# Strassen's seven products for some of mm1's ff tiles in the later chunks of a fused attention and MLP kernel

## Chip, cores, metric

One core of one Trainium2 chip. The metric is the device time of one execution in microseconds (us). "Span" is the time from the first to the last instruction in the profile; it is some 1.8 us shorter than the time of the same run (before: 305.5 and 307.26). PE is TensorE, ACT ScalarE, DVE VectorE, POOL GpSimd; PEld are PE's weight loads.

## The reference, cut

```python
def _attn_ref(q, k, v):                 # B, H, S, D = 8, 8, 576, 64
    scores = scale * np.matmul(q, k.transpose(0, 1, 3, 2))
    # heads 0-3: the last 32 positions; heads 4-7: every fourth of the last 128
    scores = np.where(masks[None, :, :, :], scores, -1000000000.0)
    ...                                 # softmax, then attn @ v
def _moe_ref(x, w_in, w_out):           # x: 4608 x 512, w_in: 512 x 2048, w_out: 2048 x 512
    h = x @ w_in
    r = np.maximum(h, 0.0)
    return ((r * r) @ w_out).astype(np.float32)
```

## The kernel before: what the argument touches

The tokens are worked in nine chunks of 512 (0 to 8). For each chunk, mm1 makes 16 "ff tiles" of h (each 128 features by 512 tokens: four matmuls of 512 columns), ACT takes the relu and DVE the square. mm2 already uses Strassen's scheme: seven products of half-size blocks, with sums of g (`sm`) and of the weights (`T`) as operands. Each chunk's work is a generator; `pump(n)` issues n of its steps. The attention of batch b is issued between the steps of chunk b - 1 (batches 2 to 7 with chunks 1 to 6), so the numbers in `pump` set the order of everything on all engines. Chunks 7 and 8 have no attention beside them.

```python
def mm1_gen(c, g, sm=None):                      # two steps for each ff tile: 32
    for ffc in range(NFF):
        ph = pmool.tile([P, TOKC], FP32, ...)    # one of 4 PSUM banks
        for n, dmk in enumerate((2, 3, 0, 1)):
            nc.tensor.matmul(ph, wi[:, dmk, ffc * P : ffc * P + P], xs[:, dmk, :], ...)
            if n == 1:
                yield
        relu_squared(c, ffc, g, ph, rts)         # ACT relu -> rt, DVE rt * rt -> g (two tiles at a time)
        ...                                      # hidden_sums: DVE, 4 operations for each half of g
        yield

def mm2_strassen_gen(c, g, sm):                  # a product is 16 matmuls of 256 columns: 4 steps
    ...
    yield from product(a, gv[:, :, 0, 0:HT], B11, True)
    s1 = part("s1")
    nc.scalar.copy(s1, a)                        # ACT reads a's bank
    yield
    d_ = bank("pod")
    yield from product(d_, gv[:, :, 1, HT:TOKC], T[:, 3], True)
    yield
    b_ = bank("pob")
    yield from product(b_, sm[:, 1], T[:, 1], True)      # needs hidden sums
    ...

for b in range(2, B):
    pending.append(moe_gen(b - 1))
    pump(1)
    ...
    pump(11)                                     # (b == 2: weight sums instead)
    for g in range(2):
        s_sliding_x(b, g)                        # scores, exponentials (ACT), masks (DVE)
        pump(7 if b == 2 and g else 5)
    s_dilated(b, 0)
    pump(5 if b == 2 else 7)
    s_dilated(b, 1)
    ...
    pump(1 if b == 2 else 6)
    cast_v(nc.scalar)                            # ACT: v to f16, vp 1.49 us, then vd twice 1.07
    ...
    pump(3)
    attn_values(b, lambda: pump(2))              # PE: AT x vp, AT x vd
    pump(1000)
```

The softmax here doesn't subtract the row's maximum and nothing guards it: scores larger than these inputs give would overflow.

Of the kernel before, what the change touches and what calls it, by code (L numbers as in the profile page):

```python
# [8 lines left out]
FP16 = mybir.dt.float16  # L9
FP32 = mybir.dt.float32  # L10
I16 = mybir.dt.int16
ALU = mybir.AluOpType
ACTF = mybir.ActivationFunctionType
P = 128
# [3 lines left out]
def kernel(  # L18
# [9 lines left out]
    nc = tc.nc  # L28

    B, H, S, D = q.shape  # L30
# [6 lines left out]
    NDM = DM // P  # L37
    NFF = DFF // P
    scale = float(1.0 / (D ** 0.5))
    TOKC = 512  # L40
    NTOKC = NTOK // TOKC
# [6 lines left out]
    PADP = P - QB  # L48
# [6 lines left out]
    const = ctx.enter_context(tc.tile_pool(name="const", bufs=1))  # L55
# [2 lines left out]
    xp = ctx.enter_context(tc.tile_pool(name="xp", bufs=4))  # L58
    gp = ctx.enter_context(tc.tile_pool(name="gp", bufs=1))
    tp = ctx.enter_context(tc.tile_pool(name="tp", bufs=1))  # L60
    osb = ctx.enter_context(tc.tile_pool(name="osb", bufs=4))
    otp = ctx.enter_context(tc.tile_pool(name="otp", bufs=3))
    papool = ctx.enter_context(tc.tile_pool(name="papool", bufs=2, space=bass.MemoryType.PSUM))
    pmool = ctx.enter_context(tc.tile_pool(name="pmool", bufs=4, space=bass.MemoryType.PSUM))
    dpool = ctx.enter_context(tc.tile_pool(name="dpool", bufs=2, space=bass.MemoryType.DRAM))
# [5 lines left out]
    xT = const.tile([P, NDM, NTOK], FP16, name="xT")  # L71
# [2 lines left out]



    QKTp = [const.tile([P, 2, PADP + S], FP16, name=f"QKTp{hp}") for hp in range(2)]
    QKTd = const.tile([P, 2, 2, KPAD + S], FP16, name="QKTd")
    QKTx = const.tile([P, 2, PADP + HH * S], FP16, name="QKTx")
    AT = const.tile([P, 8, 640], FP16, name="AT")  # L80
# [235 lines left out]
    HT = TOKC // 2  # L316
    HM = DM // 2
    NK = NFF // 2
# [19 lines left out]
    def hidden_sums(g, sm, i0, i1):  # L338
        v = g_of(g)[:, i0:i1]
        a11, a12 = v[:, :, 0, 0:HT], v[:, :, 1, 0:HT]  # L340
        a21, a22 = v[:, :, 0, HT:TOKC], v[:, :, 1, HT:TOKC]
        s1, s2, s3, s4 = (sm[:, i, i0:i1, :] for i in range(4))
        yield nc.vector.tensor_add(s1, a21, a22)
        yield nc.vector.tensor_sub(s2, s1, a11)
        yield nc.vector.tensor_sub(s3, a11, a21)
        yield nc.vector.tensor_sub(s4, a12, s2)
# [35 lines left out]
    def mm1_gen(c, g, sm=None):  # L382
        xs = xT[:, :, c * TOKC : (c + 1) * TOKC]
        rts = {}
        for ffc in range(NFF):
            ph = pmool.tile([P, TOKC], FP32, name=f"ph{c}_{ffc}", tag="pm")
            for n, dmk in enumerate((2, 3, 0, 1)):
                nc.tensor.matmul(  # L388
                    ph,
                    wi[:, dmk, ffc * P : ffc * P + P],  # L390
                    xs[:, dmk, :],
                    start=(n == 0),
                    stop=(n == NDM - 1),
                )
                if n == 1:
                    yield
            relu_squared(c, ffc, g, ph, rts)
            if sm is not None and ffc >= NFF // 2:
                if ffc == NFF // 2:
                    sums = hidden_sums(g, sm, 0, NK // 2)  # L400
                if ffc == NFF - 1:
                    sums = hidden_sums(g, sm, NK // 2, NK)
                for _ in sums:
                    if ffc < NFF - 1:
                        break
            yield

    def mm2(c, g, po, t, ffc):
        nc.tensor.matmul(  # L409
            po,  # L410
            g[:, ffc, t * P : (t + 1) * P],
            wo[:, ffc, :],
            start=(ffc == 0),
            stop=(ffc == NFF - 1),
        )
# [12 lines left out]
    def mm2_strassen_gen(c, g, sm):  # L428
        gv = g_of(g)
        T = wsum["T"]  # L430
        last = c == NTOKC - 1

        def bank(name):
            return pmool.tile([P, 2, HM], FP32, name=f"{name}{c}", tag="pm")

        def half_product(acc, lhs, rhs, t, first):
            for k in range(NK):
                nc.tensor.matmul(  # L438
                    acc,
                    lhs[:, k, t * P : (t + 1) * P],  # L440
                    rhs[:, k, :],
                    start=(first and k == 0),
                    stop=(k == NK - 1),
                    skip_group_check=True,
                )
                if k % 4 == 3 and (t, k) != (1, NK - 1):
                    yield

        def product(acc, lhs, rhs, first):
            for t in range(2):  # L450
                yield from half_product(acc[:, t, :], lhs, rhs, t, first and t == 0)

        def part(name):
            return osb.tile([P, 2, HM], FP32, name=f"{name}{c}", tag="u")

        def put(half, ot, eng, cols=slice(0, DM)):
            rows = out[c * TOKC + half * HT : c * TOKC + (half + 1) * HT, cols]
            eng.dma_start(out=rows.rearrange("(t p) m -> p t m", p=P), in_=ot[:, :, cols])  # L458

        out_eng = nc.gpsimd if c < B - 1 else nc.sync  # L460
        left, right = slice(0, HM), slice(HM, DM)
        otu = otp.tile([P, 2, DM], FP32, name=f"otu{c}", tag="ot2")
        otl = otp.tile([P, 2, DM], FP32, name=f"otl{c}", tag="ot2")
        a = bank("poa")
        yield from product(a, gv[:, :, 0, 0:HT], B11, True)
        s1 = part("s1")
        nc.scalar.copy(s1, a)
        yield
        d_ = bank("pod")
        yield from product(d_, gv[:, :, 1, HT:TOKC], T[:, 3], True)  # L470
        yield
        b_ = bank("pob")
        yield from product(b_, sm[:, 1], T[:, 1], True)
        u2 = part("u2")
        nc.vector.tensor_add(u2, b_, s1)
        yield
        yield from product(a, gv[:, :, 1, 0:HT], B21, False)
        nc.scalar.copy(otu[:, :, left], a)  # L478
        if last:
            put(0, otu, nc.sync, left)  # L480
        yield
        yield from product(b_, sm[:, 2], T[:, 2], False)
        u3 = part("u3")
        nc.vector.tensor_add(u3, b_, s1)
        nc.vector.tensor_add(otl[:, :, left], d_, u3)
        if last:
            put(1, otl, nc.sync, left)
        yield
        c_ = bank("poc")
        yield from product(c_, sm[:, 0], T[:, 0], True)  # L490

        nc.vector.tensor_add(u2, c_, u2)
        nc.vector.tensor_add(otl[:, :, right], c_, u3)  # L493
        put(1, otl, out_eng, right if last else slice(0, DM))
        yield
        if last:
            for t, eng in ((0, nc.sync), (1, nc.scalar)):
                e_ = bank(f"poe{t}_")
                yield from half_product(e_[:, 0, :], sm[:, 3], B22, t, True)
                nc.vector.tensor_add(otu[:, t, right], e_[:, 0, :], u2[:, t, :])  # L500
                r0 = c * TOKC + t * P
                eng.dma_start(out=out[r0 : r0 + P, right], in_=otu[:, t, right])
        else:
            e_ = bank("poe")
            yield from product(e_, sm[:, 3], B22, True)
            nc.vector.tensor_add(otu[:, :, right], e_, u2)
            put(0, otu, out_eng)
        yield
# [20 lines left out]
    def moe_gen(c):  # L529
        g = hidden(c)  # L530
        sm = gp.tile([P, 4, NK, HT], FP16, name=f"sm{c}", tag="sm")
        yield from mm1_gen(c, g, sm)
        yield from mm2_strassen_gen(c, g, sm)


# [6 lines left out]
    def pump(n):  # L542
        for _ in range(n):
            while pending:
                try:
                    next(pending[0])
                    break
                except StopIteration:
                    pending.pop(0)
# [430 lines left out]
# [4 lines that stand above are left out]
        if b < B - 1:  # L984

            for i in range(2):
                nc.gpsimd.tensor_copy(hold, QKTx[:, i, PADP + HH * S - 2 : PADP + HH * S - 1])
                nc.gpsimd.tensor_copy(hold, QKTd[:, i, 1, KPAD + S - 1 :])
        if 2 < b < B - 1:
            dk = keep_qk(b + 1)  # L990
        if b == 2:
            for rows, ot in late:
                nc.gpsimd.dma_start(out=rows, in_=ot)
            dk = keep_qk(b + 1)
            for _ in weight_sums():
                pump(2)
        else:
            pump(11)
        for g in range(2):
            s_sliding_x(b, g)  # L1000
            pump(7 if b == 2 and g else 5)
        s_dilated(b, 0)
        pump(5 if b == 2 else 7)
        s_dilated(b, 1)
        if b + 1 < B:
            transpose_by_dma(dk)
        pump(1 if b == 2 else 6)
        cast_v(nc.scalar)
        if b + 1 < B:
            load_v(b + 1)  # L1010
        pump(3)
        attn_values(b, lambda: pump(2))
        pump(1000)
    for c in range(B - 1, NTOKC):
# [32 lines left out]
```

## Time and profile before

| | before |
|---|---|
| time, median of 3 runs | 306.73 us (306.72 to 307.37) |
| span of the profiled run | 305.5 us, clock 1.000 |
| TensorE (PE) busy | 97% |
| chunks 2 to 6 (with attention), each | 30.87 to 30.89 us |
| chunk 7 / chunk 8 to its last matmul | 26.04 / 26.20 us |

The chunk lengths are read off the timeline: from the start of a chunk's first mm1 matmul to that of the next chunk's. The page's lines stand in the prediction.

### The profile page before, as it was taken

What the parts mean: (1) busy time and instruction counts of PE and PEld (TensorE: products, weight loads), DVE (VectorE), ACT (ScalarE), POOL (GpSimd) and SP (SyncE); (2) the same over time, 40 slices, a digit from 0 to 9 for tenths busy, and PEclk for the clock granted to TensorE, in tenths of its full rate; (3) what the DMA queues carried; (4) which work ended last, traced back from release to release, by engine and by line L of the source; (5) the groups of instructions that cost most, each with busy time, mean ns of one, the idle gap of its engine ahead of it and who ended that gap; (6) DMA issues with size and microseconds to landing.
All of it is one profiled execution on the core that took longest, in us unless ns stands there. A gap on an engine that the chain in (4) does not pass through costs nothing.

```text
span 305.5 us, 7013 instructions
## 1 busy us (share of the span) xinstructions
PE 296.3 (97%) x2898; PEld 192.8 (63%) x2898; DVE 208.8 (68%) x410; ACT 185.0 (61%) x308; POOL 48.5 (16%) x97
## 2 busy tenths in 40 slices
PE   8899998999999999999999999999999999999994
PEld 3675444444696469646964697459745974684584
DVE  4653475849966797679766977697769775843744
ACT  6466777478834893489348943894389437405610
POOL 7454013006004100320032003200100010000000
PEclk9999999999999999999999999999999999999999
DMA  8999989899899998689939983989310012003004
GB/s 175 226 213 230 233 174 203 160 232 269 210 191 219 310 170 185 217 182 198 228 111 197 216 184 123 213 184 209 117 72 0 2 61 78 2 0 137 2 0 138
DMA packets 85615, 47.89 MB, mean 157 GB/s; under 512 B 68112, under 2 KB 82896, under 8 KB 85200
## 3 DMA queue, kind: packets, MB, share of 16 engines
q1 hardware_dynamic: 76688, 27.24, 40.8%
q0 software_dynamic: 8352, 19.80, 28.9%
q8 instruction: 22, 0.36, 0.5%
q10 hardware_dynamic: 544, 0.43, 0.5%
q14 instruction: 9, 0.07, 0.1%
HBM read 39.85 MB, written 16.52 MB: 184 GB/s over the span
## 4 chain that ended last, share of the span: by engine, by line
PE 90%; ACT 3%; DMA 3%; POOL 2%; issue 1%; DVE 1%; ACTq 0%; POOLq 0%
PE ph L388 42%; PE pob L438 9%; PE poa L438 9%; PE poe L438 5%; PE poc L438 5%; PE pod L438 4%; PE po L409 4%; DMA early<-in_q_dram 3%; PE paw L776 3%; PE pav L759 2%; PE pz L675 2%; PE ps L656 1%; PE py L809 1%; PE px L791 1%; POOL early L119 1%; ACT AT L628 1%
## 5 line engine op out<-in xcount | busy, mean ns | idle before, releaser
L388 PE MATMUL ph<-xT,wi 128*128 128x512 f16 x576 | 129.8, 379 | 0.0
L354 ACT ACTIVATE rt<-ph 128x512 f16<-128x512 f32 x144 | 84.9, 601 | 36.4 <-PE ph L388 36.1
L388 PEld LDWEIGHTS <-wi 128*128 128x128 f16 x576 | 54.4, 98 | 62.4
L358 DVE TENSOR_TENSOR g<-rt 128x1024 f16<-128x1024 f16 x63 | 43.5, 691 | 47.2 <-ACT rt L354 47.0
L438 PEld LDWEIGHTS <-sm 128*128 128x128 f16 x512 | 46.9, 98 | 4.8
L438 PEld LDWEIGHTS <-g 128*128 128x128 f16 x384 | 35.9, 98 | 6.9 <-DVE g L356 1.3
L438 PE MATMUL pob<-T,sm 128*128 128x256 f16 x256 | 32.5, 272 | 0.0
L438 PE MATMUL poa<-wo,g 128*128 128x256 f16 x256 | 32.4, 273 | 0.0
L458 POOL DMA_DIRECT2D out_dram<-otl x6 | 4.6, 763 | 152.6 <-DVE otl L493 152.6
L815 ACT COPY xT<-py 128x576 f16<-128x576 f16 x16 | 10.2, 640 | 27.3 <-PE py L809 27.3
L740 DVE TENSOR_TENSOR x_d<-paw,rcp_d 72x512 f16<-72x512 f32 x32 | 22.0, 687 | 1.1
L797 ACT COPY xT<-px 128x576 f16<-128x576 f16 x16 | 10.3, 642 | 13.6 <-PE px L791 13.6
L409 PE MATMUL po<-wo,g 128*128 128x512 f16 x64 | 17.8, 379 | 0.0
L735 DVE RECIPROCAL rcp_d<-paw 72x8 f32<-72x8 f32 x32 | 6.4, 199 | 16.2 <-PE paw L776 16.2
L628 ACT ACTIVATE AT<-pz 128x576 f16<-128x576 f32 x28 | 16.6, 652 | 1.0 <-PE pz L675 0.6
L628 ACT ACTIVATE AT<-ps 128x576 f16<-128x576 f32 x28 | 16.6, 649 | 0.5
L740 DVE TENSOR_TENSOR x_p<-pav,rcp_p 96x512 f16<-96x512 f32 (+1 forms) x24 | 16.2, 676 | 0.8
L438 PE MATMUL poe<-wo,sm 128*128 128x256 f16 x128 | 16.3, 273 | 0.0
L438 PE MATMUL pod<-T,g 128*128 128x256 f16 x128 | 16.3, 272 | 0.0
L438 PE MATMUL poc<-T,sm 128*128 128x256 f16 x128 | 16.2, 272 | 0.0
L478 ACT COPY otu<-poa 128x512 f32<-128x512 f32 x8 | 4.7, 586 | 17.5 <-PE poa L438 17.5
L629 DVE TENSOR_TENSOR AT<-AT,maskd 128x576 f16<-128x576 f16 x28 | 12.2, 455 | 3.5 <-ACT AT L628 2.5
(120 smaller groups left out, 354.5 us busy)
## 6 DMA issues: line engine op xcount, KB each, us to landing
sv<-in_v_dram SPq DMA_DIRECT2D x40, 128.0 KB, 3.1
sd<-in_v_dram SPq DMA_DIRECT2D x8, 512.0 KB, 6.2
dk<-in_k_dram POOLq DMA_DIRECT2D x12, 288.0 KB, 7.0
dk<-in_q_dram POOLq DMA_DIRECT2D x12, 288.0 KB, 7.5
out_dram<-otl POOLq DMA_DIRECT2D x6, 512.0 KB, 3.3
out_dram<-otu POOLq DMA_DIRECT2D x6, 512.0 KB, 4.2
sd<-in_v_dram SPq DMA_DIRECT2D x8, 288.0 KB
wi<-in_moe_w_in_dram POOLq DMA_DIRECT2D x4, 512.0 KB, 10.3
```

The lines of the kernel that those rows point to most:

```text
L354: nc.scalar.activation(rt[:, o, :], ph[:], ACTF.Relu)
L358: nc.vector.tensor_mul(g[:, ffc - 1 : ffc + 1, :], rt, rt)
L388: nc.tensor.matmul(ph, wi[:, dmk, ffc * P : ffc * P + P], xs[:, dmk, :], start=(n == 0), stop=(n == NDM - 1),)
L409: nc.tensor.matmul(po, g[:, ffc, t * P : (t + 1) * P], wo[:, ffc, :], start=(ffc == 0), stop=(ffc == NFF - 1),)
L438: nc.tensor.matmul(acc, lhs[:, k, t * P : (t + 1) * P], rhs[:, k, :], start=(first and k == 0), stop=(k == NK - 1), skip_group_check=True,)
L628: nc.scalar.activation(AT[:, u, 0:UW], ps[:, :, 0 : UW // 2], ACTF.Exp, scale=scale)
L629: nc.vector.tensor_mul(AT[:, u, 0:UW], AT[:, u, 0:UW], mask)
L735: nc.vector.reciprocal(rcp[0:w, 0:n], pv[:, :, :, D])
L740: nc.vector.tensor_tensor(out=x[0:w, 0:n], in0=pv[:, :, :, 0:D], in1=rcp[0:w, 0:n].unsqueeze(3).to_broadcast([w, n, HH, D]), op=ALU.mult,)
L776: nc.tensor.matmul(pav[:, e, h * (D + 2) : h * (D + 2) + D + 1], AT[:, u, off : off + P], vd[:, t, 2 * a + e, h, 0 : D + 1], start=True, s ...
L797: nc.scalar.copy(xT[:, 0:2, t0 : t0 + 288], px[:, 0:UW].rearrange("x (c t) -> x c t", c=2),)
L815: nc.scalar.copy(xT[:, 2:4, t0 : t0 + 288].rearrange("x c (i r) -> x c i r", r=DIL), py[:, 0:UW].rearrange("x (c r i) -> x c i r", c=2, r= ...
```

## The change

Its intent: a unit of Strassen's seven products computes four ff tiles from 28 matmuls of 256 columns in place of 16 of 512, one eighth fewer columns. Chunks 3 to 6 get one unit each (a quarter of their tiles), chunks 7 and 8 two. The price is sums of x and of the weights, and the combining of products, on DVE and ACT. Cut to its core (allocations left out, lines joined):

```diff
+    units = {**{c: 1 for c in range(3, NTOKC - 2)}, NTOKC - 2: 2, NTOKC - 1: 2}
+    # w_in_sums: 8 DVE operations, once, in chunk 2; x_sums(c): 4 DVE operations (t1..t4) per chunk
+    def unit_gen(c, u, g):
+        product(a, w(0, 0), x_quarter(c, 0, 0), True)
+        m1 = part("m1"); nc.scalar.copy(m1, a)
+        yield
+        product(e, w(0, 1), x_quarter(c, 1, 0), True)
+        nc.vector.tensor_add(g1[:, :, first], e, m1)
+        yield "stage"
+        product(a, s2, t2, False)                          # goes on adding in bank a
+        m6 = part("m6"); nc.scalar.copy(m6, a)
+        yield
+        product(d, s1, t1, True)
+        finish(g1[:, :, first])                            # ACT relu, DVE square, in place
+        yield "stage"
+        product(a, s3, t3, False)
+        m7 = part("m7"); nc.scalar.copy(m7, a)
+        nc.vector.tensor_add(g2[:, :, second], d, m7)
+        yield "stage"
+        product(a, w(1, 1), t4, False)
+        nc.scalar.activation(g2[:, :, first], a, ACTF.Relu)
+        yield
+        product(d, s4, x_quarter(c, 1, 1), False)          # must wait for the addition d + m7
+        nc.vector.tensor_mul(g2[:, :, first], g2[:, :, first], g2[:, :, first])
+        nc.vector.tensor_add(g1[:, :, second], d, m6)
+        yield "stage"
+        finish(g2[:, :, second]); finish(g1[:, :, second])
+
+    orders = {                       # 0, 1: a stage of that unit; p: a plain tile; s: one hidden sum
+        1: "0p0p0p0p0" + "p" + "sp" * 4 + "ppp",
+        2: "p01010p10p10p1psspspsp",
+    }
     ... chunk 7's mm2 takes its sixth and fifth products later; output buffers 3 -> 2
-            pump(11)
+            pump(14 if b - 1 in units else 11)
     ...
-        pump(1 if b == 2 else 6)
+        pump(1 if b == 2 else 5 if b - 1 in units else 6)
         cast_v(nc.scalar)
     ...
-        pump(3)
+        pump(1 if b - 1 in units else 3)
         attn_values(b, lambda: pump(2))
```

More of the change, by code (lines that the diff above doesn't have):

```diff
@@ L60 @@
     tp = ctx.enter_context(tc.tile_pool(name="tp", bufs=1))
+    kp = ctx.enter_context(tc.tile_pool(name="kp", bufs=1))
     osb = ctx.enter_context(tc.tile_pool(name="osb", bufs=4))
-    otp = ctx.enter_context(tc.tile_pool(name="otp", bufs=3))
+    otp = ctx.enter_context(tc.tile_pool(name="otp", bufs=2))
     papool = ctx.enter_context(tc.tile_pool(name="papool", bufs=2, space=bass.MemoryType.PSUM))
@@ L73 @@
     wo = wpool.tile([P, NFF, DM], FP16, name="wo")
-    QKTp = [const.tile([P, 2, PADP + S], FP16, name=f"QKTp{hp}") for hp in range(2)]
+    QKTp = [kp.tile([P, 2, PADP + S], FP16, name=f"QKTp{hp}", tag=f"k{hp}") for hp in range(2)]
     QKTd = const.tile([P, 2, 2, KPAD + S], FP16, name="QKTd")
@@ L406, in mm1_gen, with w_in_sums, quarter @@
             yield
+    units = {**{c: 1 for c in range(3, NTOKC - 2)}, NTOKC - 2: 2, NTOKC - 1: 2}
+    HU = 2 * P
+    ws = [const.tile([P, 4, 2, HU], FP16, name=f"ws{u}") for u in range(2)]
+    def w_in_sums(u):
+        def quarter(i, j):
+            f0 = 4 * P * u + HU * i
+            return wi[:, 2 * j : 2 * j + 2, f0 : f0 + HU]
+        s1, s2, s3, s4 = (ws[u][:, i] for i in range(4))
+        yield nc.vector.tensor_add(s1, quarter(1, 0), quarter(1, 1))
+        yield nc.vector.tensor_sub(s2, s1, quarter(0, 0))
+        yield nc.vector.tensor_sub(s3, quarter(0, 0), quarter(1, 0))
+        yield nc.vector.tensor_sub(s4, quarter(0, 1), s2)
@@ new lines, with x_quarter, x_sums @@
+    xsums = {}
+    def x_quarter(c, j, i):
+        t0 = c * TOKC + HT * i
+        return xT[:, 2 * j : 2 * j + 2, t0 : t0 + HT]
+    def x_sums(c):
+        t = [kp.tile([P, 2, 2, HT], FP16, name=f"xs{c}_{n}", tag=f"k{n}") for n in range(2)]
+        t1, t2, t3, t4 = t[0][:, 0], t[0][:, 1], t[1][:, 0], t[1][:, 1]
+        xsums[c] = t1, t2, t3, t4
+        nc.vector.tensor_sub(t1, x_quarter(c, 0, 1), x_quarter(c, 0, 0))
+        nc.vector.tensor_sub(t2, x_quarter(c, 1, 1), t1)
+        nc.vector.tensor_sub(t3, x_quarter(c, 1, 1), x_quarter(c, 0, 1))
+        nc.vector.tensor_sub(t4, x_quarter(c, 1, 0), t2)
@@ new lines, in unit_gen, with w, product, part @@
+    def unit_gen(c, u, g):
+        t1, t2, t3, t4 = xsums[c]
+        s1, s2, s3, s4 = (ws[u][:, i] for i in range(4))
+        f0 = 4 * u
+        g1, g2 = g[:, f0 : f0 + 2, :], g[:, f0 + 2 : f0 + 4, :]
+        first, second = slice(0, HT), slice(HT, TOKC)
+        def w(i, j):
+            c0 = P * f0 + HU * i
+            return wi[:, 2 * j : 2 * j + 2, c0 : c0 + HU]
+        def product(acc, lhs, rhs, start):
+            for n in range(2):
+                for k in range(2):
+                    nc.tensor.matmul(
+                        acc[:, n, :],
+                        lhs[:, k, n * P : (n + 1) * P],
+                        rhs[:, k, :],
+                        start=(start and n == 0 and k == 0),
+                        stop=(k == 1),
+                        skip_group_check=True,
+                    )
+        def part(name):
+            return osb.tile([P, 2, HT], FP32, name=f"{name}{c}_{u}", tag="u")
+        a = papool.tile([P, 2, HT], FP32, name=f"pu{c}_{u}", tag="pa")
+        def finish(x):
+            nc.scalar.activation(x, x, ACTF.Relu)
+            nc.vector.tensor_mul(x, x, x)
+        product(a, w(0, 0), x_quarter(c, 0, 0), True)
+        m1 = part("m1")
+        nc.scalar.copy(m1, a)
+        yield
+        e = pmool.tile([P, 2, HT], FP32, name=f"pe{c}_{u}", tag="pm")
+        product(e, w(0, 1), x_quarter(c, 1, 0), True)
+        nc.vector.tensor_add(g1[:, :, first], e, m1)
+        yield "stage"
+        product(a, s2, t2, False)
+        m6 = part("m6")
+        nc.scalar.copy(m6, a)
+        yield
+        d = pmool.tile([P, 2, HT], FP32, name=f"pq{c}_{u}", tag="pm")
+        product(d, s1, t1, True)
+        finish(g1[:, :, first])
+        yield "stage"
+        product(a, s3, t3, False)
+        m7 = part("m7")
+        nc.scalar.copy(m7, a)
+        nc.vector.tensor_add(g2[:, :, second], d, m7)
[7 more added lines that the diff above has]
+        yield "stage"
+        finish(g2[:, :, second])
+        finish(g1[:, :, second])
@@ new lines, with mm1_units_gen @@
+    orders = {
+        1: "0p0p0p0p0" + "p" + "sp" * 4 + "ppp",
+        2: "p01010p10p10p1psspspsp",
+    }
+    def mm1_units_gen(c, g, sm, nu):
+        if c not in xsums:
+            x_sums(c)
+        xs = xT[:, :, c * TOKC : (c + 1) * TOKC]
+        rts = {}
+        stages = [unit_gen(c, u, g) for u in range(nu)]
+        sums = hidden_sums(g, sm, 0, NK // 2)
+        ffc = 4 * nu
+        for step in orders[nu]:
+            if step == "p":
+                ph = pmool.tile([P, TOKC], FP32, name=f"ph{c}_{ffc}", tag="pm")
+                for n in range(NDM):
+                    nc.tensor.matmul(
+                        ph,
+                        wi[:, n, ffc * P : ffc * P + P],
+                        xs[:, n, :],
+                        start=(n == 0),
+                        stop=(n == NDM - 1),
+                    )
+                    if n == 1:
+                        yield
+                relu_squared(c, ffc, g, ph, rts)
+                ffc += 1
+                yield
+            elif step == "s":
+                next(sums)
+            else:
+                for what in stages[int(step)]:
+                    yield
+                    if what:
+                        break
+        assert ffc == NFF
+        for _ in sums:
+            pass
+        for _ in hidden_sums(g, sm, NK // 2, NK):
+            pass
+        yield
@@ L471, in mm2_strassen_gen, with sixth, fifth @@
         yield
-        b_ = bank("pob")
-        yield from product(b_, sm[:, 1], T[:, 1], True)
-        u2 = part("u2")
-        nc.vector.tensor_add(u2, b_, s1)
-        yield
+        def sixth():
+            b_ = bank("pob")
+            yield from product(b_, sm[:, 1], T[:, 1], True)
+            u2 = part("u2")
+            nc.vector.tensor_add(u2, b_, s1)
+            yield
+            return b_, u2
+        def fifth(u2):
+            c_ = bank("poc")
+            yield from product(c_, sm[:, 0], T[:, 0], True)
+            nc.vector.tensor_add(u2, c_, u2)
+            return c_
+        relaxed = c == NTOKC - 2
+        if not relaxed:
+            b_, u2 = yield from sixth()
         yield from product(a, gv[:, :, 1, 0:HT], B21, False)
@@ L481, in mm2_strassen_gen @@
         yield
+        if relaxed:
+            b_, u2 = yield from sixth()
+            c_ = yield from fifth(u2)
+            yield
         yield from product(b_, sm[:, 2], T[:, 2], False)
@@ L487, in mm2_strassen_gen @@
             put(1, otl, nc.sync, left)
-        yield
-        c_ = bank("poc")
-        yield from product(c_, sm[:, 0], T[:, 0], True)
-        nc.vector.tensor_add(u2, c_, u2)
+        if not relaxed:
+            yield
+            c_ = yield from fifth(u2)
         nc.vector.tensor_add(otl[:, :, right], c_, u3)
         put(1, otl, out_eng, right if last else slice(0, DM))
+        if c + 1 == NTOKC - 1:
+            x_sums(c + 1)
         yield
@@ L531, in moe_gen @@
         sm = gp.tile([P, 4, NK, HT], FP16, name=f"sm{c}", tag="sm")
-        yield from mm1_gen(c, g, sm)
+        if c in units:
+            yield from mm1_units_gen(c, g, sm, units[c])
+        else:
+            yield from mm1_gen(c, g, sm)
         yield from mm2_strassen_gen(c, g, sm)
@@ L996 @@
                 pump(2)
+        elif b == 3:
+            for u in range(2):
+                for _ in w_in_sums(u):
+                    pump(1)
+            pump(3)
         else:
-            pump(11)
+            pump(14 if b - 1 in units else 11)
         for g in range(2):
```

## The prediction

> **What bounds the kernel now.** I read the page's busy shares and its chain first. TensorE (PE) is busy for 97% of the span, and the chain that ended last is PE for 90%.
>
> ```profile
> PE 296.3 (97%) x2898; PEld 192.8 (63%) x2898; DVE 208.8 (68%) x410; ACT 185.0 (61%) x308; POOL 48.5 (16%) x97
> PE 90%; ACT 3%; DMA 3%; POOL 2%; issue 1%; DVE 1%; ACTq 0%; POOLq 0%
> ```
>
> Then I cut the span at the chunk borders that the chain in order of time shows, and asked for each engine's busy time per chunk:
>
> ```profile
> 156.88:187.76 30.88, 30.88 (x318) 20.78 (x316) 23.53 (x45) 20.24 (x33) 4.64 (x10) 1.00 0.79 182
> 249.50:275.54 26.04, 26.04 (x178) 17.23 (x176) 14.75 (x23) 10.72 (x18) 1.45 (x2) 1.00 0.11 41
> ```
>
> The first is chunk 4 with batch 5's attention beside it; the second is chunk 7, which has no attention. The columns are the stretch, its length, then busy time of PE, PEld, DVE, ACT and POOL, granted clock and DMA share. PE never rests in either, so matmul columns removed there come off the time one for one, and any new PE wait is added one for one. DVE has 7 us to spare beside attention, ACT 10.6. How fast PE runs comes from the chain in order of time:
>
> ```profile
> 249.50 13.81 PE ph L388 x64
> 263.32 1.75 PE poa L438 x16
> ```
>
> A 512-column matmul takes 13.81/64 = 0.2158 us, a 256-column one 1.75/16 = 0.1092 us.
>
> Since other engines must feed PE, I took the durations of their operations from the groups by shape (busy us, mean ns):
>
> ```profile
> L354 ACT ACTIVATE rt<-ph 128x512 f16<-128x512 f32 x144 | 84.9, 601 | 36.4 <-PE ph L388 36.1
> L358 DVE TENSOR_TENSOR g<-rt 128x1024 f16<-128x1024 f16 x63 | 43.5, 691 | 47.2 <-ACT rt L354 47.0
> L356 DVE TENSOR_TENSOR g<-rt 128x512 f16<-128x512 f16 x18 | 7.5, 424 | 1.8 <-ACT rt L354 1.2
> L475 DVE TENSOR_TENSOR u<-pob,s 128x512 f32<-128x512 f32 x8 | 5.5, 691 | 3.2 <-PE pob L438 3.2
> ```
>
> Last the order in time where attention's values start, in chunk 4:
>
> ```profile
> 170.75 0.43 PE L675 MATMUL pz<-QKTd 64*128 64x72 f16 x16
> 171.10 1.19 ACT L628 ACTIVATE AT<-pz 128x576 f16<-128x576 f32 x2
> 172.18 1.09 ACT L354 ACTIVATE rt<-ph 128x512 f16<-128x512 f32 x2
> 172.43 2.02 PE L438 MATMUL poa<-wo,g 128*128 128x256 f16 x16
> 173.13 1.49 ACT L166 CAST vp<-sv 128x1536 f16<-128x1536 f32 x1
> 174.29 1.04 PE L438 MATMUL pod<-T,g 128*128 128x256 f16 x8
> 175.16 0.42 PE L759 MATMUL pav<-vp,AT 128*128 128x65 f16 x8
> 176.39 0.62 ACT L467 COPY s<-poa 128x512 f32<-128x512 f32 x1
> ```
>
> The cast of v ends at 174.62, 0.54 us before PE wants it at 175.16. The copy of s1 runs at 176.39, though its product was done at 174.29: ACT keeps the program's order. In chunk 1, where the last scores stand closer to the values, the cast is already late:
>
> ```profile
> 80.99 1.47 ACT L166 CAST vp<-sv 128x1536 f16<-128x1536 f32 x1
> 82.52 0.42 PE L759 MATMUL pav<-vp,AT 128*128 128x65 f16 x8 [0.66 <-ACT vp L166]
> ```
>
> [...] two halves cost only 1% more than one whole. [...] 512 columns take 691 ns from PSUM and 424 in f16. [...] The trace has 601, and the pair at 172.18 starts 1.09 - 0.60 = 0.49 apart. DVE's starts are 0.61 apart for 0.69 us operations (chunk 7: 273.83, 274.44), and about 0.36 for the 424 ns ones. PE's last issue to the start on ACT is 0.20 us (pod issued at 264.90, s1 copied at 265.10), ACT to DVE 0.03, either to PE 0.05.
>
> **The change, part by part.** One unit computes four ff tiles of one chunk. It removes 16 matmuls of 512 (3.45 us) and adds 7 × 4 = 28 of 256 (3.06): 0.395 us less PE. There are 4 units in chunks 3 to 6 and 4 in chunks 7 and 8: **8 × 0.395 = 3.2 us**, which is the ceiling of the whole change (1.0%).
>
> It adds per unit on ACT three copies and four relus for four relus: 3 × 0.5 = 1.5 us. On DVE three PSUM additions and four half squares for two whole squares: 3 × 0.61 + 4 × 0.36 - 2 × 0.61 = 2.0 us. Each of six chunks adds four x differences, 1.4 us of DVE; chunk 2 adds eight weight sums, 2.9. These fit beside PE on average; what matters is the order.
>
> Step A, inside a unit (chunks 3 to 6; time from the chunk's start). DVE does the previous output add at 0.20, then the x differences, free at 2.25. t2 is ready at 1.6, just before PE wants it at 1.74. The first product's addition therefore starts at 2.25 and ends at 2.94; the relu on it holds ACT at 2.97, the second plain tile's relu starts at 3.66. The third product into bank a (s3 × t3) ends at 3.91; its copy m7 runs on ACT 4.17 to 4.77; the addition d + m7 on DVE 4.90 to 5.59. PE meanwhile does one plain tile and the next product and wants to go on accumulating into d at about 5.2, but must wait for that read: **0.4 to 0.5 us in each of four chunks, 1.8 in all**.
>
> Step B, the values. The change pumps 3 steps more before the first scores, and takes 1 and 2 back around the cast. Counting the generator's steps (15 for the unit with four tiles, 16 for eight tiles, 1 at the end = 32, as before), the last dilated scores now come after step 32, not 29, and the cast is emitted after step 37, not 35. Step 36 holds the copy of s1, so the cast now stands behind it in ACT's queue. That copy waits for the end of product a (call it E): starts at E + 0.20, the cast at E + 0.70, ends at E + 2.19. PE wants the values after two blocks of pod, E + 0.87, and waits to E + 2.24: **1.35 us in each of four chunks, 5.4 in all**.
>
> Step C, the end of mm1. DVE's backlog (x differences, unit additions, half the hidden sums) makes the square of ff tile 14 late. Walking DVE's queue in chunks 3 to 6 it ends at about 16.45, PE wants it at 16.13: 0.3 each. In chunks 7 and 8 DVE is busy without a break from 9.3; the square ends at 15.1, PE wants it at 14.5 to 14.6: 0.6 each. Together 2.4.
>
> Step D, two units interleaved (chunks 7, 8). The fifth plain tile gets, if the four banks go round in order, the second unit's d. Its last reader stands behind the square of a relu of the fourth product: product end + 0.25 + 0.60 + 0.39 + 0.69 + 0.05 = 2.0 us, where PE has d's last product and a tile to do, 1.3: 0.65 each, 1.3 in all.
>
> Sum: 306.7 - 3.2 + 5.4 + 1.8 = 310.7 from the parts that I trust, and 3.7 more from C and D, which hang on a few tenths in queues; I count half, 1.85. **Predicted 312.6 us.**
>
> **Rivals.** R1: the matmuls saved arrive whole, 303.6, or most of them, up to 306. For it: PE is the bound; two engines have room on average; the order of chunk 7's second half was changed to give late sums more time, which looks like tuning against a profile. Against: step B follows from program order and the cast's 1.49 us, and chunk 1 already shows that wait. R2: DVE becomes the bound beside attention. Its busy time would be 23.5 + 2.6 + 1.7 = 27.8 of 30.5 us, with late masks and hidden sums and A and C twice as large: about 316. Against: back-to-back starts are closer than durations, so the real load is some 80%. R3: the two output buffers instead of three make an output wait for its store. Stores land in 3 to 4 us and the buffer is wanted 20 us later, so nothing: the time stays at the sum.
>
> **Range and chances.** Without B and half of A the time would be about 306.5, the low end; with C and D whole and a little more, 316. Faster by 2% (under 300.6) is below the ceiling's reach: 0.01. The border to slower is 312.9, near my point: I give 0.55 to same, since R1 has some weight, and 0.44 to slower.
>
> **What would show it.** B is right if the waits list PE's pav (or its weight load) behind ACT's vp for 1.2 to 1.5 us in four chunks, with the s1 copy directly ahead of the cast; wrong if that wait is under 0.5. A: PE's d product waits on the DVE addition with m7, 0.3 to 0.6. C: poa's eighth weight load waits on the square. D: a plain tile in the last two chunks waits 0.5 or more. The chunks should last 30.5 + 2 in 3 to 6 and 25.3 + 1.2 in 7 and 8. PE's busy records should fall by some 3 us in any case; if the span falls as much, A to D are all wrong.

The marked cuts are general statements that no trace or run of this case shows. The sum: 306.7 - 3.2 + 5.4 + 1.8 + 1.85 = 312.55, put as 312.6. The spacing of 0.1092 us comes from starts: in chunk 7 mm2's seven products take from 263.15 to 275.38, 12.23 / 112, and 2 × 0.1092 / 0.2158 = 1.012 is the "1%". The 691 and 424 ns are DVE's and the 601 ns ACT's, as listed by shape above. "About 0.36" is high: the two half squares at 40.21 last 0.75 us together, so they start 0.33 apart. The 0.03 is a relu that ended at 263.09 and its square at 263.12 (chunk 7); the 0.05, chunk 1's cast, which ended at 82.46, and its values at 82.52. "Some 80%" was an estimate, from starts 0.61 apart for operations of 0.69: 27.8 × 0.61 / 0.69 = 24.6 of 30.5 us. The page's median for an output store is 3.3 us (`otl`) and 4.2 (`otu`); `otl`'s store was issued at 156.96 and the next chunk's `otl` written from 183.99, 27 us later.

## The result and the profile after

The changed kernel takes **313.81 us** (median, 313.46 to 314.41, 4 runs) against 306.73: ratio 1.023, 95% interval 1.0205 to 1.0256. Ratios here are the mean time of one kernel's fast runs over that of the other's fast runs of the same rounds, so not quite the ratio of the medians. The profiled run: span 312.3 us, clock 0.998.

The changed kernel's page, busy shares and the chain that ended last by engine:

```profile
PE 295.9 (95%) x2994; PEld 201.9 (65%) x2994; DVE 235.6 (75%) x482; ACT 193.4 (62%) x332; POOL 47.6 (15%) x97
PE 81%; ACT 6%; DVE 6%; DMA 2%; issue 2%; POOL 1%; ACTq 0%; POOLq 0%
```

The chain now runs through ACT and DVE for 12% of the span, where it was 4%: PE waits. Busy time per chunk, for chunk 4 and chunk 7 (stretch, length, PE, PEld, DVE, ACT, POOL, clock, DMA share, GB/s):

```profile
158.35:190.59 32.24, 30.82 (x331) 21.88 (x329) 26.86 (x54) 21.38 (x36) 4.30 (x10) 1.00 0.81 175
255.24:281.98 26.74, 25.68 (x201) 19.49 (x200) 19.60 (x37) 12.71 (x24) 1.45 (x2) 1.00 0.11 41
```

Chunk 4 went from 30.87 to 32.24 us although its matmuls became fewer in columns; DVE still has 5.4 us to spare. Chunk 7 went from 26.04 to 26.74. All chunks together, 4 × 1.37 + 0.70 + 0.71 = 6.9 us, account for the difference of the spans (6.8; the stretch ahead of chunk 1 is 0.3 us longer, the one after the last matmul 0.3 shorter). Chunk 2, with its eight weight sums more on DVE, stayed at 30.87.

The waits of PE in the changed kernel (us in total, times, longest):

```profile
PE pav L922 <- ACT vp L168: 5.3, 5, 1.2
PE poa L580 <- DVE g L358: 1.3, 2, 0.7
PE pq L457 <- DVE g L494: 1.0, 4, 0.3
PE poa L580 <- DVE g L360: 0.8, 2, 0.4
```

Four waits of `pav` are new (the fifth is chunk 1's, as before). A wait is shown too short here: a 256-column record lasts 0.27 us where the next starts 0.109 later, so the record of the matmul ahead covers about 0.16 us of each gap. I therefore measure a gap from starts: start of the next group, less start of the group before, less its matmuls × 0.1092 (or 0.2158).

The values in chunk 4, in order of time (start, duration, engine, line, operation; in brackets how long the engine was idle before, and what ended it):

```profile
174.16 1.95 PE L580 MATMUL poa<-wo,g 128*128 128x256 f16 x16
174.40 1.19 ACT L791 ACTIVATE AT<-pz 128x576 f16<-128x576 f32 x2
175.95 1.04 PE L580 MATMUL pod<-T,g 128*128 128x256 f16 x8
176.15 0.59 ACT L609 COPY s<-poa 128x512 f32<-128x512 f32 x1 [0.57 <-PE poa L580]
176.63 1.48 ACT L168 CAST vp<-sv 128x1536 f16<-128x1536 f32 x1
178.16 0.42 PE L922 MATMUL pav<-vp,AT 128*128 128x65 f16 x8 [1.17 <-ACT vp L168]
```

Before, the cast stood ahead of the s1 copy and 0.54 us ahead of need. Now ACT idles 0.57 us for the product, copies s1, and only then casts. PE has done its 8 matmuls of `pod` at 175.95 + 0.87 = 176.82 and starts the values at 178.16: a gap of 1.34 us.

Inside the unit of the same chunk:

```profile
162.60 0.58 ACT L493 COPY m<-pu 128x512 f32<-128x512 f32 x1
163.23 0.60 PE L457 MATMUL pu<-xs,wi 128*128 128x256 f16 x4
163.34 0.68 DVE L494 TENSOR_TENSOR g<-pq,m 128x512 f16<-128x512 f32 x1
164.08 0.60 PE L457 MATMUL pq<-xT,ws 128*128 128x256 f16 x4 [0.25 <-DVE g L494]
```

The last product into d (`pq`) could start at 163.23 + 0.44 = 163.67 and starts at 164.08, when DVE's addition has read d: 0.41 us.

And the end of mm1 in chunk 7:

```profile
267.33 0.69 DVE L345 TENSOR_TENSOR sm<-g 128x1024 f16<-128x1024 f16 x1
268.05 0.69 DVE L346 TENSOR_TENSOR sm<-sm,g 128x1024 f16<-128x1024 f16 x1
268.18 0.82 PE L580 MATMUL poa<-wo,g 128*128 128x256 f16 x6
268.66 0.68 DVE L360 TENSOR_TENSOR g<-rt 128x1024 f16<-128x1024 f16 x1
269.26 0.69 DVE L347 TENSOR_TENSOR sm<-g 128x1024 f16<-128x1024 f16 x1
269.40 0.28 PE L580 MATMUL poa<-wo,g 128*128 128x256 f16 x1 [0.41 <-DVE g L360]
269.87 0.42 DVE L358 TENSOR_TENSOR g<-rt 128x512 f16<-128x512 f16 x1
270.34 1.16 PE L580 MATMUL poa<-wo,g 128*128 128x256 f16 x9 [0.65 <-DVE g L358]
```

PE stops at the seventh and again at the eighth matmul of mm2's first product, each time for a square (L360, L358) ahead of which DVE does hidden sums (`sm`) that PE needs only later. The product takes from 268.18 to 271.33, where the next begins: 3.15 us for 1.75 us of work, a gap of 1.40.

### The profile page after: what moved, and what is told of

Its sections match the earlier page's. It is cut to its first block, busy times and chain, and to the rows that moved or that the text cites. A ratio compares the mean times of both kernels' runs of the same rounds, so it can differ in the third digit from the quotient of the medians.

```text
span 312.3 us, 7296 instructions
## 1 busy us (share of the span) xinstructions
PE 295.9 (95%) x2994; PEld 201.9 (65%) x2994; DVE 235.6 (75%) x482; ACT 193.4 (62%) x332; POOL 47.6 (15%) x97
## 4 chain that ended last, share of the span: by engine, by line
PE 81%; ACT 6%; DVE 6%; DMA 2%; issue 2%; POOL 1%; ACTq 0%; POOLq 0%
PE ph L524 14%; PE ph L390 14%; PE pob L580 9%; PE poa L580 9%; PE poe L580 4%; PE poc L580 4%; PE po L551 4%; PE pu L457 3%; PE pod L580 3%; ACT vp L168 3%; PE paw L939 3%; DMA early<-in_q_dram 2%; PE pq L457 2%; PE pav L922 2%; DVE g L360 2%
## 5 line engine op out<-in xcount | busy, mean ns | idle before, releaser
L356 ACT ACTIVATE rt<-ph 128x512 f16<-128x512 f32 x112 | 64.9, 615 | 28.3 <-PE ph L524 17.9
L524 PE MATMUL ph<-xT,wi 128*128 128x512 f16 x256 | 61.2, 379 | 0.0
L360 DVE TENSOR_TENSOR g<-rt 128x1024 f16<-128x1024 f16 x47 | 32.4, 688 | 19.4 <-ACT rt L356 19.3
L390 PE MATMUL ph<-xT,wi 128*128 128x512 f16 x192 | 43.1, 379 | 0.0
L524 PEld LDWEIGHTS <-wi 128*128 128x128 f16 x256 | 24.0, 98 | 23.1
L390 PEld LDWEIGHTS <-wi 128*128 128x128 f16 x192 | 18.2, 98 | 21.1
```

Source lines behind the costliest of these rows:

```text
L356: nc.scalar.activation(rt[:, o, :], ph[:], ACTF.Relu)
L360: nc.vector.tensor_mul(g[:, ffc - 1 : ffc + 1, :], rt, rt)
L524: nc.tensor.matmul(ph, wi[:, n, ffc * P : ffc * P + P], xs[:, n, :], start=(n == 0), stop=(n == NDM - 1),)
```

## The experiments

The theory was the prediction's: saving 3.2 us, lost to three orders, A inside the unit, B at the values, C at the end of mm1 (D, a bank, showed no gap). The main rival was that DVE, at 26.9 of 32.2 us, is in truth the bound, and that the waits only show where its load happens to surface. Eight kernels ran, all correct, each beside runs of the kernel before (medians 306.80 to 307.01; e8 on another chip than the rest, so its ratio is the fair figure).

| run | time, us | ratio to before (95%) | chunk 4, us | chunk 7, us |
|---|---|---|---|---|
| before | 306.73 | | 30.87 | 26.04 |
| the change | 313.81 | 1.023 (1.0205 to 1.0256) | 32.24 | 26.74 |
| e1_pumps_only | 312.00 | 1.0174 (1.0159 to 1.0189) | 32.09 | 26.03 |
| e2_tail_only | 308.32 | 1.0047 (1.003 to 1.0064) | 30.87 | 26.74 |
| e3_cast_first | 309.82 | 1.0103 (1.0088 to 1.0119) | 31.35 | 26.75 |
| e4_scores_back | 310.64 | 1.0123 (1.0108 to 1.0138) | 31.46 | 26.74 |
| e5_split_unit | 311.88 | 1.0173 (1.0156 to 1.019) | 31.89 | 26.74 |
| e6_tail_late_sums | 305.35 | 0.995 (0.9935 to 0.9965) | 30.87 | 25.33 |
| e7_all_mended | 305.80 | 0.9971 (0.9957 to 0.9985) | 31.00 | 25.33 |
| e8_sums_in_mm2 | 303.88 | 0.9894 (0.9877 to 0.9912) | 30.54 | 25.34 |

### B without any Strassen: e1_pumps_only

```diff
 # the kernel before
-            pump(11)
+            pump(14 if 4 <= b else 11)
-        pump(1 if b == 2 else 6)
+        pump(1 if b == 2 else 5 if 4 <= b else 6)
-        pump(3)
+        pump(1 if 4 <= b else 3)
```

> The kernel before with nothing of Strassen in mm1: only the change's three new step counts around attention (14 for 11, 5 for 6, 1 for 3, batches 4 to 7). Theory B (the cast of v stands behind the s1 copy in ACT's queue and the values come too soon after the last scores): the values wait 1.2 to 1.4 us in each of four chunks, so the time is 306.7 + 5.2 = 311.9 (311.2 to 312.6). Rival (DVE or ACT is overloaded by the units' own additions, and the wait for the cast is only where that load shows): with no units there is no load, 306.7 to 307.5.

Measured 312.00 us. In chunk 4 the order in time is the changed kernel's:

```profile
173.52 1.92 PE L438 MATMUL poa<-wo,g 128*128 128x256 f16 x16
175.48 0.59 ACT L467 COPY s<-poa 128x512 f32<-128x512 f32 x1 [0.54 <-PE poa L438]
175.96 1.48 ACT L166 CAST vp<-sv 128x1536 f16<-128x1536 f32 x1
177.49 0.41 PE L759 MATMUL pav<-vp,AT 128*128 128x65 f16 x8 [1.17 <-ACT vp L166]
```

The same wait of 1.17 us stands there with no unit and no extra load, and the chunk is 1.22 us longer than in the kernel before: the 1.34 us gap, less 0.11 us by which mm2's first product had waited before and no longer does. Three step counts alone cost 5.2 us. The load rival falls for this wait.

### The last two chunks alone: e2_tail_only

```diff
 # the changed kernel
-    units = {**{c: 1 for c in range(3, NTOKC - 2)}, NTOKC - 2: 2, NTOKC - 1: 2}
+    units = {NTOKC - 2: 2, NTOKC - 1: 2}
```

> The changed kernel with units in chunks 7 and 8 alone; chunks 3 to 6 and the step counts there are as before. Theory: each of the last two chunks loses 1.4 us at its first mm2 product (late squares) and 0.1 inside the units, and saves 0.79, so +0.7 each: 306.7 + 1.4 = 308.1 (307.6 to 308.6). Rival (the saving arrives where no attention stands beside it, and the loss is all in chunks 3 to 6): 305.2.

Measured 308.32 us; chunks 7 and 8 as in the changed kernel (26.74 and 26.91), chunks 3 to 6 as before. The last two chunks lose by themselves, with no attention beside them.

### The queue's order: e3_cast_first and e4_scores_back

```diff
 # e3: the changed kernel, the cast issued after step 35, not 37
-        pump(1 if b == 2 else 5 if b - 1 in units else 6)
+        pump(1 if b == 2 else 3 if b - 1 in units else 6)
-        pump(1 if b - 1 in units else 3)
+        pump(3)
 # e4: the changed kernel, scores after steps 15, 19, 23, 29; cast 35; values 38
-            pump(7 if b == 2 and g else 5)
+            pump(7 if b == 2 and g else 4 if b - 1 in units else 5)
-        pump(5 if b == 2 else 7)
+        pump(5 if b == 2 else 6 if b - 1 in units else 7)
-        pump(1 if b == 2 else 5 if b - 1 in units else 6)
+        pump(1 if b == 2 else 6)
-        pump(1 if b - 1 in units else 3)
+        pump(3)
```

> The changed kernel with one thing moved: the cast of v is issued after step 35 and not 37, so it stands ahead of the s1 copy in ACT's queue; the values still come after step 38 and the scores stay where the change put them. Theory B: the cast starts right after the two exponentials of the last scores, about 0.5 us after their last start, and ends 1.49 later, so the wait of the values falls from 1.34 to about 0.3 us in four chunks: 313.8 - 4.1 = 309.7 (309.0 to 310.4). Rival (ACT is simply loaded up to there, whatever the order): under 1 us gained, 313.

Measured 309.82 us. Chunk 4, the cast and the values:

```profile
173.83 1.48 ACT L168 CAST vp<-sv 128x1536 f16<-128x1536 f32 x1
175.36 0.42 PE L922 MATMUL pav<-vp,AT 128*128 128x65 f16 x8
```

The gap ahead of the values fell from 1.33 to 0.17 us. Of the 1.16 gained, 0.27 came back: the third group of values now has a gap of 0.27 us.

> The changed kernel with its units, but the scores pulled back so that the last ones come after step 29 as before, the cast after step 35 and the values after 38 (scores after steps 15, 19, 23, 29 in place of 15, 20, 25, 32). Theory B: the wait of the values goes away whole, 313.8 - 5.4 = 308.4 (307.7 to 309.4, the upper part if the closer scores wait for their banks). Rival (DVE is the bound beside attention): the wait moves to another place and the time stays over 312.

Measured 310.64 us, outside the expected 307.7 to 309.4. The wait for the cast is gone whole, but the scores, now closer together, wait behind ACT's exponentials: in chunk 4 the second half of the first dilated scores has a gap of 0.34 us (0.22 shown), and the third group of values one of 0.16. 32.24 - 1.34 + 0.34 + 0.16 = 31.40, measured 31.46. So moving scores is a worse mending of B than moving the cast; and part of B's cost does return elsewhere, as the rival had it, though 0.5 of 1.34 us only.

### A: e5_split_unit

```diff
 # the changed kernel
         nc.scalar.activation(g2[:, :, first], a, ACTF.Relu)
-        yield
+        yield "stage" if c < NTOKC - 2 else None
-        1: "0p0p0p0p0" + "p" + ...
+        1: "0p0p0p0p00" + "p" + ...
```

> The changed kernel with step A's wait taken away: in chunks 3 to 6 the unit's last two products are parted, so that a plain ff tile (0.86 us) lies between the addition d + m7 that DVE must finish and the product that goes on in d; the first scores follow after the same 15 steps. Theory A: the 0.41 us gap before that product goes in four chunks, nothing else moves (the cast still stands behind the s1 copy): 313.8 - 1.6 = 312.2 (311.8 to 312.6), chunks of 31.83 us in place of 32.24. Rival (the gap is DVE's load and comes back at the next wait): 313.4 to 313.9.

Measured 311.88 us, chunks 3 to 6 at 31.88 to 31.89. The gap of 0.41 us before `pq` is gone from chunk 4, and 0.05 of it is found at mm2's first product (0.09 for 0.04). A is a matter of order as well.

### C: e6_tail_late_sums

```diff
 # e2_tail_only
-        2: "p01010p10p10p1psspspsp",
+        2: "p01010p10p10p1pppp",
 ...
-        for _ in sums:
-            pass
-        for _ in hidden_sums(g, sm, NK // 2, NK):
+        rest = hidden_sums(g, sm, NK // 2, NK)
+        for _ in sums:
+            next(rest)
+        for _ in rest:
             pass
```

> The run with units in chunks 7 and 8 alone, and one order changed in them: DVE's eight hidden sums come after the last squares, not between them. Theory (C: the squares are late because DVE[...] does sums ahead of them): the 1.4 us gap in the first mm2 product goes, each of the two chunks lasts 25.35 us in place of 26.74, 308.3 - 2.8 = 305.5 (305.2 to 306.0, the upper part if the sums are now late for the second or third product); faster than the kernel before by some 0.4%. Rival (ACT is behind with the relus, whatever DVE does first): the gap stays above 0.7 us and the time over 307.

The cut is a general claim about DVE; what the changed kernel's trace shows is the square at 268.66, behind sums at 267.33 and 268.05, though its relus had ended by 267.80.

Measured 305.35 us, chunk 7 at 25.33 us. The end of its mm1:

```profile
262.35 1.91 PE L581 MATMUL poa<-wo,g 128*128 128x256 f16 x16
262.61 0.99 DVE L358 TENSOR_TENSOR g<-rt 128x512 f16<-128x512 f16 x2
263.52 1.29 DVE L345 TENSOR_TENSOR sm<-g 128x1024 f16<-128x1024 f16 x2
264.09 1.91 PE L581 MATMUL pod<-T,g 128*128 128x256 f16 x16
```

The squares come first, the product starts every 0.109 us and ends after 1.74. DVE's work is the same, its order is not. The rival that ACT's relus were late falls. This version beats the kernel before by 0.5%.

### Everything mended: e7_all_mended and e8_sums_in_mm2

```diff
 # e7: e5's and e6's edits with the units of the change, and
+        if b - 1 in units:
+            cast_sliding_v(nc.scalar, NB)          # vp ahead of the last exponentials
         s_dilated(b, 1)
 ...
-        cast_v(nc.scalar)
+        ...                                        # there, only vd for those batches
 # e8: e7, and for chunks with one unit, at the end of mm1
+        if nu == 1:
+            next(rest); next(rest)                 # two of the last four sums
+            later[c] = rest                        # two after mm2's third product
```

> The whole change, with all three orders mended: the parted products (A), the cast of the sliding v ahead of the last scores' exponentials in ACT's queue (B), the sums after the squares in the last two chunks (C). Theory: nothing but the orders was wrong, so most of the 3.2 us arrives: chunks 3 to 6 at 30.6 us (30.5 to 30.8), the last two at 25.35, together 306.7 - 1.2 - 1.4 = 304.1 (303.7 to 305.3). Rival (with units beside attention, DVE and ACT are too full and the waits move elsewhere): no faster than the run with units in the last two chunks alone, 305.5 or more.

Measured 305.80 us, not the 303.7 to 305.3 expected. Chunks 7 and 8 did what they should (25.33); chunks 3 to 6 came to 31.00 us, not 30.6. In chunk 4:

```profile
175.16 0.69 DVE L348 TENSOR_TENSOR sm<-g,sm 128x1024 f16<-128x1024 f16 x1
176.73 0.69 DVE L904 TENSOR_TENSOR x_p<-pav,rcp_p 96x512 f16<-96x512 f32 x1
177.47 0.43 PE L923 MATMUL pav<-vp,AT 128*128 128x65 f16 x8 [0.27 <-DVE x_p L904]
```

The third group of values needs the bank of the first, which DVE's `x_p` reads; that operation stood behind hidden sums that mm2 wants much later. From starts the gap is 0.44 us, the whole of the miss. In the changed kernel, where PE comes later because of the cast, this wait does not appear (`x_p` ended at 179.54, the third group started at 180.41).

> The run with all three orders mended, and one more: in chunks 3 to 6 the last two hidden sums, which mm2 needs only for its fifth and seventh products, are issued after mm2's third product and not at the end of mm1. In the run before, the third group of values waits 0.35 us for a bank whose reader on DVE stands behind those two sums (0.6 each). Theory: that gap goes, chunks of 30.65 us in place of 31.00, so 305.8 - 1.4 = 304.4 (304.0 to 305.2), under the 305.35 of the units in the last two chunks alone. Rival (DVE is simply full beside attention, and the two sums make a later operation late instead): 305.5 to 306.

Measured **303.88 us** (303.43 to 304.19, 6 runs), ratio 0.9894, a little under the expected 304.0 to 305.2: chunks 3 to 6 at 30.54 to 30.55, 0.33 us less than before, which is the 0.395 us of columns less the 0.07 that the unit's second stage waits for its x difference `t2`. The third group of values in chunk 4 now starts when its turn comes (175.81 + 8 × 0.1092 = 176.68). These two lines are followed by the page's busy shares:

```profile
175.81 1.03 PE L587 MATMUL pob<-T,sm 128*128 128x256 f16 x8
176.68 0.42 PE L931 MATMUL pav<-vp,AT 128*128 128x65 f16 x8
PE 293.3 (97%) x2994; PEld 201.4 (67%) x2994; DVE 232.8 (77%) x482; ACT 193.6 (64%) x332; POOL 47.5 (16%) x97
```

PE's waits behind `pq`, `poa` and the four late casts are gone from the list. No work was taken from DVE or ACT between the change and e8 (482 and 332 instructions in both), only its order was changed: the rival "DVE is the bound" falls as a whole. Not run: the mended orders on the kernel before. Its chunks 3 to 6 have one comparable wait, the 0.11 us in mm2's first product, so they could have gained little there. The change's whole ceiling, 3.2 us, is nearly reached (2.9 from the medians against 306.73, 3.1 against the 307.01 of the same rounds).

## Why the prediction was right, point by point

It said 312.6 us, chances 0.55 for within 2% and 0.44 for slower; the time was 313.81, 1.2 us more and over the border of 312.9, so the likelier class did not come. Per chunk, from starts:

| step | predicted gap | measured in the changed kernel | tested by |
|---|---|---|---|
| saving | 0.395 per unit | 0.33 net in chunk 4, 0.71 net of two units in chunk 7, with the waits of A to C gone (0.07 at `t2` and 0.09 at `pq` stay) | e8, e6 |
| A | 0.4 to 0.5 | 0.41; also 0.08 at `t2`, not predicted | e5 (the 0.41) |
| B | 1.35 | 1.33 to 1.34 | e1, e3 |
| C, chunks 3 to 6 | 0.3 | 0.04 | not needed |
| C, chunks 7 and 8 | 0.6 | 1.40 | e6 |
| D | 0.65 | 0 | seen in the trace |

- **Saving, A and B** were right in mechanism and in size. B came from counting the generator's steps and from the order of issue on ACT, which idled 0.57 us ahead of the s1 copy with the cast behind it, and is half of the new waits. Added up: -3.2 for the columns, 2.0 for A and `t2`, 5.3 for B, 3.0 for C, 0.2 for 0.09 at `pq` in chunks 7 and 8, less 0.4 for the old wait of 0.11 in mm2's first product, are 6.9 us, as the chunks show. That the three small terms that the prediction did not have (0.3 at `t2`, 0.2 at `pq`, -0.4) nearly cancel is luck.
- **C and D** were both wrong, D in its assumption and C in its size, in opposite directions. D assumed that "the four banks go round in order". They do not; the program, built again, gives these banks in chunk 7, in order of allocation (no trace shows banks):

```
tile (p = plain, e/d = unit's bank)   p1 e0 e1 d0 d1 p2 p3 p4 p5 p6
PSUM bank                              4  7  6  5  4  7  6  7  6  5
```

The fifth plain tile gets bank 6, which the third had left before (its relu ended at 263.79, the fifth starts at 264.72), and not d1's bank 4. The trace agrees with that: it shows no gap after the last product of the units, and five tiles run in one piece:

```profile
263.43 0.60 PE L457 MATMUL pq<-xT,ws 128*128 128x256 f16 x4
263.86 4.48 PE L524 MATMUL ph<-xT,wi 128*128 128x512 f16 x20
```

PE therefore reaches mm2 at 268.18 - 255.07 = 13.11 us into the chunk, and would want tile 14, the eighth matmul, 7 × 0.1092 = 0.76 later, at 13.87; the prediction had 14.5 to 14.6. DVE's square of tile 14 ended at 270.29 - 255.07 = 15.22; the prediction had 15.1. The walk of DVE's queue was right, PE was some 0.7 us earlier, and what D did not cost, C did: 0.6 + 0.7 = 1.3 of the 1.40. This exchange is not chance: DVE's square, ended at 270.29, fixed when PE went on, 270.34, however PE had waited before.
- **C beside attention** did not come: the square ended at 174.90, PE wanted it at 174.16 + 0.76 = 174.92. From the chunk's start these are 16.55 and 16.57, where the prediction had 16.45 and 16.13: DVE was 0.1 us later, PE 0.44. Most of PE's part is some 0.10 us ahead of each of the four score groups, where 128-row matmuls give way to 64-row ones (the first: 164.51 + 4 × 0.2158 = 165.37, started at 165.47), which I had left out; its cause was not tested. The kernel before has the same (0.10 to 0.11); the prediction read "PE never rests" from busy records, which cover such gaps.
- **The half count** of C and D was the mis-sized term: 3.7 us in the walk, counted 1.85, measured 2 × 1.40 + 4 × 0.04 = 3.0. With that, 310.7 + 3.0 = 313.7. The half was a guess and no reading of the profile; taken whole, C and D would have given 314.4, which is nearer, though the 0.3 in each of chunks 3 to 6 did not come.
- **The rivals.** R2 (DVE bound) is refuted by e8. Its load was also too high: 2.6 us per unit does not follow from the durations listed (3 × 0.69 + 4 × 0.42 - 2 × 0.69 = 2.4), and DVE's busy time came to 26.9 us, not 27.8. R3 (two output buffers) costs nothing: e8 keeps the two buffers and shows no such wait. R1 was wrong for this order of issue and right for a better one.
- **A check that failed:** I wrote that PE's busy time would fall by some 3 us in any case. It fell from 296.3 to 295.9. One reason is that the records are longer than the spacing and cover 0.16 us of each gap: chunk 4 has 0.395 us fewer columns and two large gaps more, and its busy time fell by 0.05 only (30.87 to 30.82). In e8, with those gaps gone, it fell to 293.3, by the 3.0 forecast. So where PE waited, its busy time did not show the columns saved: 0.05 us of 0.395.

## What to carry to other kernels

In this kernel, with PE busy for 97% of the span, a saving of 3.2 us of columns arrived (2.9 in e8) only when no operation in the order of ACT or DVE became late; the changed kernel lost 7.1 us instead. So list for each new order what stands ahead of the operation that the bound engine waits for, and by how much it was early before. Counting the steps and adding durations from the profile gave the wait of B to 0.02 us here; where two long walks had to be set against each other, as in C, the result was off by 0.3 to 0.8 us. If a good change loses, mend the order before giving it up: the same products, casts and sums gave 313.8 us in one order and 303.9 in another.
